# Order of the first transfers in a Fourier-mixing and SoLU kernel on one core: Q and g_ln behind the first pair's x, g_ln loaded in rows, third chunk ahead of the last piece of w_in

## The chip, the cores and the metric

The kernel runs on one core of one Trainium2 chip. The metric is the device time of one execution in microseconds (us), as the median of several runs. Engines are named as in the profile: PE (TensorE, with PEld for its weight loads), DVE (VectorE), ACT (ScalarE), POOL (GpSimd), SP (SyncE). SP and POOL issue the transfers; in the profile "SPq" is SP's queue and "POOLq" POOL's.

## The reference, cut to what matters

```python
# x: (8, 3136, 256), w_in: (256, 1024), w_out: (1024, 256), g_ln: (1024,), all float32
X = np.fft.fft(np.fft.fft(x, axis=1), axis=2).real          # Fourier mixing over sequence and features
h = X.reshape(25088, 256) @ w_in
e = np.exp(h - h.max(-1, keepdims=True))
solu = h * e / (e.sum(-1, keepdims=True) + 1e-9)
ln = (solu - solu.mean(-1)) / sqrt(var(solu) + 1e-6) * g_ln
out = ln @ w_out
```

## The kernel before, in words

The kernel treats two sequences at a time, so there are four pairs. The sequence transform of 3136 points is split into 49 x 64. Its first step (`transform1`, line 215) multiplies rows of x, folded by their symmetries, with the table F. The half-results go through DRAM (`keep` writes `zd`, `turn` reads it back as `g`), and the second step (`transform2`, line 243) uses the table T. The feature transform is not made on the data. It is multiplied into w_in once at the start: with Q, the 256 x 257 table of the feature transform, `product_in` (line 685) makes Wi = Q x w_in in PSUM and `keep_in` (line 689) copies it out. The column `w_mid` comes from `mid` (line 676: two ScalarE copies that read Q's last column) and a third product.

After that, 100 units (25 per pair) run through `up` (line 279), `even`, `join`, `expo`, `product`, `square`, a turn of blocks and the down product (line 462). This loop takes the span from about 58 us to the end.

All of the program's order is written out by hand (`tc.manual_schedule`): the calls in the main function are the order of each engine's instructions. A tile framework only adds the waits. The start, which the change touches, is as follows.

- **The first pair's x.** It comes in 8 chunks of four columns. For chunk c, `load` issues two transfers: `xa` from SP (line 126, 98 rows of 4 KB, 392 KB) and the mirrored rows `xb` from POOL (line 128, a gather by the index table `idx`, as large). Chunks 0, 1, 6 and 7 use two rotating buffers; chunks 2 to 5 lie in "rooms", tiles that serve another purpose later, so that their transfers can start at once. `add_mirror` (lines 143 and 145) adds xb to xa on VectorE, `fold` (lines 150, 151, 163) folds the features into `y` (two buffers), and `transform1` then runs on TensorE in two steps of four matmul passes, each with a ScalarE copy (line 218).
- **w_in in four pieces.** The weights are given to the chip as 32-bit words of wider numbers in this program: a piece of 128 x 4 KB (`piece_in`, line 581, 512 KB) is turned into float32 by `exponent_in` (line 584 on VectorE, then `confine`, three ScalarE steps at lines 608, 610, 612) and `narrow_in` (lines 584, 625, 628, 634 on VectorE). Pieces 0 to 3 must all be converted before the first product with Q.
- **w_out** is treated likewise later (`load_out` line 700, `exponent_out`, `narrow_out`), with g_ln multiplied in at line 634. g_ln is scaled by 2^-20 in `scale_out` (line 704, ScalarE).
- **The queue.** Transfers that SP issues run in order on one queue, those that POOL issues on another. SP has eight completion counters that it uses in turn, so the issue of a transfer also waits for the one issued eight places earlier. SP's order at the start is: idx, piece 0, piece 1, xa of chunk 0, F, piece 2, chunk 1, piece 3, chunk 2, chunk 3, Q, g_ln, chunk 4, chunk 5, chunk 6, then stores, x0, chunk 7 and w_out as they become due.

On VectorE the order in the first 50 us is: exponents of pieces 0 and 1, narrowing of 0 and 1, exponent of 2, chunk 0, narrowing of 2, exponent of 3, chunk 1, narrowing of 3, chunks 2 to 7, then w_out. On TensorE it is: chunks 0 to 3, the product with Q for the even half (8 steps), chunk 4, a quarter of the odd half's product, chunk 5, another quarter, chunks 6 and 7, the rest. Before chunk 3's transform ScalarE does `mid` and `scale_out`.

Of the kernel before, what the change touches and what calls it, by code (L numbers as in the profile page):

```python
# [9 lines left out]
FP32 = mybir.dt.float32  # L10
# [7 lines left out]
P = 128  # L18


N1, N2 = 49, 64
NK = N1 // 2 + 1
NH = N2 // 2
PR = 2 * N1
ZR = 4 * NK
CH = 4
NC = NH // CH
# [11 lines left out]
def shared(b, n):  # L39

    return WHOLE // 2 <= b < n - 1 and all(u % NK for u in (2 * b, 2 * b + 1))
# [3 lines left out]
def kernel(  # L45
# [19 lines left out]
    nc = tc.nc  # L65
    B, S, D = x.shape
    FF = moe_w_in.shape[1]
    KF = FF // P
# [4 lines left out]
    x_g = x.rearrange("b (n1 g l) d -> (b n1 g) (l d)", n1=N1, l=CH)  # L73
    x_pn = x.rearrange("b (n1 n2) d -> (b n1) n2 d", n2=N2)
# [3 lines left out]
    xpool = ctx.enter_context(tc.tile_pool(name="xpool", bufs=2))  # L78
# [6 lines left out]
    fpool = ctx.enter_context(tc.tile_pool(name="fpool", bufs=2))  # L85
# [3 lines left out]
    F = const.tile([PR, 6, ZR], FP32, name="F")  # L89
# [6 lines left out]
    ident = const.tile([P, P], FP32, name="ident")  # L96
    neg_half = const.tile([P, 2], FP32, name="neg_half")
    idx = const.tile([P, NP * (NC + NK)], I32, name="idx")
    w_mid = const.tile([P, FF], FP32, name="w_mid")
    g_ln = const.tile([P, KF], FP32, name="g_ln")  # L100
# [17 lines left out]
    def load(pr, c, room=None):  # L118

        r = slice(pr.p * PR, (pr.p + 1) * PR)  # L120
        if room is None:
            xa = xpool.tile([PR, CH, D], FP32, tag="xa", name="xa")
            xb = xpool.tile([PR, CH, D], FP32, tag="xb", name="xb")
        else:
            xa, xb = (t.rearrange("p (l d) -> p l d", d=D) for t in room)
        nc.sync.dma_start(out=xa, in_=x_pn[r, c * CH + 1 : (c + 1) * CH + 1, :])
        i = pr.p * NC + c
        nc.gpsimd.indirect_dma_start(
            out=xb.rearrange("p l d -> p (l d)"), out_offset=None, in_=x_g,
            in_offset=bass.IndirectOffsetOnAxis(ap=idx[0:PR, i : i + 1], axis=0))  # L130
        x0 = None
        if c == NC - 1:
            x0 = xpool.tile([PR, 1, D], FP32, tag="x0", name="x0", bufs=1)
            nc.sync.dma_start(out=x0, in_=x_pn[r, 0:1, :])
        pr.raw[c] = (xa, xb, x0)

    def add_mirror(pr, c, engine, part=None):

        xa, xb, _ = pr.raw[c]
        rows = (0, CH) if part is None else (part * CH // 2, (part + 1) * CH // 2)  # L140
        r = slice(rows[0], min(rows[1], CH - 1 if c == NC - 1 else CH))
        a, rb = xa[:, r, :], xb[:, ::-1, :][:, r, :]
        i = engine.tensor_tensor(out=a[:, :, 1:D], in0=a[:, :, 1:D], in1=rb[:, :, D - 1 : 0 : -1], op=ALU.add)
        if part is None:
            engine.tensor_tensor(out=a[:, :, 0:1], in0=a[:, :, 0:1], in1=rb[:, :, 0:1], op=ALU.add)
        return i
# [6 lines left out]
    def fold(pr, c):  # L153

        xa, _, x0 = pr.raw.pop(c)
        pr.y[c] = xpool.tile([PR, CH, D], FP32, tag="y", name="y")
        sides = [(pr.y[c], xa)]
        if c == NC - 1:
            pr.y0 = xpool.tile([PR, 1, D], FP32, tag="y0", name="y0", bufs=1)
            sides.append((pr.y0, x0))  # L160
        for o, i in sides:
            fold_features(o, i)
            nc.vector.tensor_copy(out=o[:, :, 0:129:128], in_=i[:, :, 0:129:128])  # L163
# [473 lines left out]
    class Weights:  # L637
# [24 lines left out]
        def load_tables(self):  # L662
            self.Q = fpool.tile([P, KD, D + 1], FP32, tag="ev", name="Q", bufs=1)
            nc.sync.dma_start(out=self.Q, in_=q_tab.rearrange("(c p) d -> p c d", p=P))
            nc.sync.dma_start(out=g_ln, in_=moe_g_ln.rearrange("(c p) -> p c", p=P))

        def load_table(self, i):
            k1 = slice(KG, NK) if i else slice(0, KG)
# [32 lines left out]
                                  in_=moe_w_out.bitcast(I32).rearrange("(c p) f -> p c f", p=P)[:, c])  # L701

        def scale_out(self):
            nc.scalar.mul(out=g_ln, in_=g_ln, mul=2.0 ** -20)

        def exponent_out(self, i):
            self.units.append(exponent(moe_w_out, self.raw[:, 2 * i * NW : 2 * (i + 1) * NW]))
# [76 lines left out]
    with tc.manual_schedule():  # L784
        pairs = [Pair(p) for p in range(NP)]
        first, weights = pairs[0], Weights()
# [3 lines left out]
        rooms = {}  # L790
        for c in range(2, 6, 2):
            room = fpool.tile([P, 2, KF, 4, 64], FP32, tag="uT", name="room", bufs=2)
            room = room[0:PR].rearrange("p w c i m -> p (w c i m)").rearrange("p (a n) -> p a n", a=4)
            rooms[c], rooms[c + 1] = [room[:, i] for i in (0, 1)], [room[:, i] for i in (2, 3)]
        weights.load_in()
        for c in range(4):
            weights.piece_in(c)
            if c:
                load(first, c - 1, rooms.get(c - 1))
            if c == 1:  # L800
                nc.sync.dma_start(out=F, in_=f_tab)
        load(first, 3, rooms[3])
        weights.load_tables()
        for c in range(4, 6):
            load(first, c, rooms[c])
        nc.vector.memset(ones, 1.0)
        nc.vector.memset(neg_half, -0.5)
        bits(top_bit, neg_half[:, 0:1].bitcast(I32), 31, ALU.logical_shift_right, 31, ALU.logical_shift_left)
# [6 lines left out]
        for c in range(NC):  # L815

            if c == 0:
                weights.narrow_in(0)
                weights.narrow_in(1)
            elif c < 3:  # L820
                weights.narrow_in(c + 1)
            if c < 2:
                weights.exponent_in(c + 2)
            add_mirror(first, c, nc.vector)
            fold(first, c)
            if c == NC - 1:
                for i in range(2):
                    weights.exponent_out(i)
                confine(weights.units[0], True)
                weights.narrow_out(0)  # L830
            if c + 6 < NC:
                load(first, c + 6)
            if c == 3:
                weights.place_out()
                for i in range(2):
                    weights.load_out(i)
                weights.load_table(0)
                weights.mid()
                weights.scale_out()
            for s in range(CH // 2):  # L840
                if c == NC - 1:
                    confine(weights.units[0], parts=(s,))
                transform1(first, c * CH // 2 + s)
            if c == 3:
                weights.keep_in(0, weights.product_in(0))
            elif c == 4:
                odd = weights.product_in(1, (0,))
            elif c == 5:
                weights.product_in(1, (1,), odd)
# [136 lines left out]
        for i in range(whole + 1, len(units) + lag + 1):  # L986
# [84 lines left out]
            if i in (len(units), len(units) + 1):  # L1071
                w = i - len(units)
# [7 lines left out]
def _tables(B, S, D):  # L1080

    import numpy as np

    def cs(num, den):
        a = 2.0 * math.pi * (num % den) / den
        return np.cos(a), np.sin(a)

    n1, k1 = np.arange(N1)[:, None], np.arange(NK)[None, :]
    c, s = cs(n1 * k1, N1)
    cm, sm = cs((n1 - N1 // 2) * k1, N1)  # L1090
    zero = np.zeros_like(c)
    tabs = [(c, s), (s, -c), (c, zero), (s, zero), (zero, cm), (zero, sm)]
    f = np.zeros((2, N1, 6, NK, 2, 2))
    for t, (u, v) in enumerate(tabs):
        for b in range(2):
            f[b, :, t, :, b, 0], f[b, :, t, :, b, 1] = u, v
    k = (np.arange(NK)[:, None] + N1 * np.arange(N2)[None, :])[None]
    n2 = (np.arange(NH) + 1) % NH
    c, s = cs(n2[:, None, None] * k, S)
    t = np.stack([c, -s])  # L1100
    t[1, -1] = 1.0 - 2.0 * (k[0] % 2)
    m, d = np.arange(D)[:, None], np.arange(D)[None, :]
    q = np.where(d <= D // 2, cs(m * d, D)[0], -cs(m * (d - D // 2), D)[1])

    q = np.concatenate([q, q[:, D // 2 : D // 2 + 1]], axis=1)
    q[:, D // 2] = 0.0
    sign = np.where(np.arange(P) == 0, 1.0, -1.0)[:, None]
    row = np.arange(B)[:, None] * N1 + np.arange(N1)[::-1]

    load = row.reshape(-1, PR, 1) * (N2 // CH) + N2 // CH - 1 - np.arange(NC)  # L1110
    mirror = np.zeros((P, B // 2 * (NC + NK)), np.int32)
    mirror[:PR, : B // 2 * NC] = load.transpose(1, 0, 2).reshape(PR, -1)
    rows = np.arange(B)[:, None, None] * S + (N1 - np.arange(NK)) + N1 * np.arange(N2)[::-1, None]
    rows = rows.reshape(B // 2, P, NK).transpose(1, 0, 2).reshape(P, -1)
    for b in range(rows.shape[1] // 2):
        if shared(b, rows.shape[1] // 2):

            two = rows[:, 2 * b : 2 * b + 2].reshape(2, 2, 32, 2).transpose(1, 0, 3, 2)
            rows[:, 2 * b : 2 * b + 2] = two.reshape(2, P).T
    mirror[:, B // 2 * NC :] = rows  # L1120
    return {
        "f_tab": f.reshape(PR, 6, ZR).astype(np.float32),
        "t_tab": t.reshape(2 * NH, NK, N2).astype(np.float32),
        "q_tab": q.astype(np.float32),
        "sign": sign.astype(np.float32),
        "mirror": mirror,
    }
# [32 lines left out]
```

## Time and profile before

| | us |
|---|---|
| median of 3 runs | 1126.72 (1125.56 to 1128.06) |
| the profiled execution, its own time | 1127.41 |
| its span, first to last instruction | 1125.6 |
| TensorE busy | 1093.1 (97%) |
| VectorE busy | 980.5 (87%) |
| ScalarE busy | 798.2 (71%) |
| GpSimd busy | 807.5 (72%) |

Times in the profile count from the span's start. A line of the timeline gives start, duration, engine, source line, operation, the tile written and the tile read, how many instructions are merged, and in brackets how long the engine was idle before and what ended the idle time. A line of the waits gives the engine, the tile and line that waited, what ended the wait, the total in us, how often, and the longest.

### The profile page before, as it was taken

What the parts mean: (1) busy time and instruction counts of PE and PEld (TensorE: products, weight loads), DVE (VectorE), ACT (ScalarE), POOL (GpSimd) and SP (SyncE); (2) the same over time, 40 slices, a digit from 0 to 9 for tenths busy, and PEclk for the clock granted to TensorE, in tenths of its full rate; (3) what the DMA queues carried; (4) which work ended last, traced back from release to release, by engine and by line L of the source; (5) the groups of instructions that cost most, each with busy time, mean ns of one, the idle gap of its engine ahead of it and who ended that gap; (6) DMA issues with size and microseconds to landing.
All of it is one profiled execution on the core that took longest, in us unless ns stands there. A gap on an engine that the chain in (4) does not pass through costs nothing. (4 is left out here: it accounts for less than half of the span.)

```text
span 1125.6 us, 22002 instructions
## 1 busy us (share of the span) xinstructions
PE 1093.1 (97%) x7030; PEld 874.1 (78%) x7030; DVE 980.5 (87%) x1440; ACT 798.2 (71%) x1946; POOL 807.5 (72%) x707
## 2 busy tenths in 40 slices
PE   1999999999999999999999999999999999999998
PEld 1556888787787787878877787878877788778888
DVE  6899889888889888898888988898988899888984
ACT  3578777777766777777767777777776777777771
POOL 3048888776887888865878788876776676766665
PEclk9999999999999999999999999999999999999999
DMA  9773798766978889766889797876786785865665
GB/s 236 211 205 82 172 188 202 175 148 152 176 174 167 194 181 187 195 146 144 158 165 183 173 192 181 200 179 143 154 154 143 141 163 125 157 144 112 142 133 126
DMA packets 458569, 185.77 MB, mean 165 GB/s; under 512 B 425774, under 2 KB 440374, under 8 KB 458456
## 3 DMA queue, kind: packets, MB, share of 16 engines
q1 hardware_dynamic: 444568, 145.96, 62.3%
q0 software_dynamic: 13888, 38.42, 13.2%
q8 instruction: 57, 0.93, 0.4%
q14 instruction: 56, 0.46, 0.1%
HBM read 44.78 MB, written 38.80 MB: 74 GB/s over the span
## 5 line engine op out<-in xcount | busy, mean ns | idle before, releaser
L279 PE MATMUL ps_h<-Wi,q 128*128 128x512 f32 x800 | 361.6, 593 | 0.5 <-DVE nmax L300 0.2
L455 POOL TENSOR_TENSOR S<-uT 128x512 f32<-128x512 f32 x186 | 237.3, 1276 | 107.1 <-DVE u L315 35.8
L462 PE MATMUL ps_m<-Ws,S 128*128 128x128 f32 x2304 | 296.0, 275 | 0.0
L462 PEld LDWEIGHTS ps_m<-Ws,S 128*128 128x128 f32 x2304 | 279.5, 192 | 3.2 <-issue 0.2
L322 ACT ACTIVATE h<-u,usum 128x1024 f32<-128x1024 f32 x196 | 225.0, 1148 | 72.3 <-DVE u L315 72.3
L279 PEld LDWEIGHTS ps_h<-Wi,q 128*128 128x128 f32 x800 | 144.2, 190 | 145.0 <-issue 141.9
L315 DVE SCALAR_TENSOR_TENSOR u<-h,u 128x1024 f32<-128x1024 f32 x196 | 233.8, 1228 | 10.9 <-ACT u L308 10.8
L308 ACT ACTIVATE u<-h,nmax 128x1024 f32<-128x1024 f32 x196 | 223.3, 1141 | 2.3 <-DVE nmax L300 1.1
L386 DVE STREAM_TRANSPOSE v<-u 128x2048 f32<-128x2048 f32 x88 | 203.4, 2311 | 3.1
L462 PE MATMUL ps_m<-Wo,uT 128*128 128x128 f32 x1536 | 203.7, 276 | 0.0
L462 PEld LDWEIGHTS ps_m<-Wo,uT 128*128 128x128 f32 x1536 | 187.9, 192 | 1.2 <-issue 1.2
L300 DVE CUSTOM_DVE_ANT_0 h<-ev,ps_h 128x1024 f32<-128x1024 f32 x100 | 122.1, 1221 | 17.1 <-DVE ev L292 9.2
L549 POOL DMA_INDIRECT out_dram<-ot,idx x96 | 111.1, 1157 | 30.0 <-issue 12.8
L300 DVE CUSTOM_DVE_ANT_0 h<-h,ps_h 128x1024 f32<-128x1024 f32 x96 | 117.2, 1221 | 14.6 <-DVE nmax L300 0.7
L455 POOL TENSOR_TENSOR S<-uT,S 128x512 f32<-128x512 f32 x93 | 118.8, 1277 | 7.2
L455 POOL TENSOR_TENSOR S<-S,uT 128x512 f32<-128x512 f32 x93 | 118.6, 1276 | 7.3
L292 DVE SCALAR_TENSOR_TENSOR ev<-w_mid,r,ps_h 128x1024 f32<-128x1024 f32 x99 | 122.8, 1241 | 0.9 <-PE ps_h L279 0.7
L462 PE MATMUL ps_m<-Ws,uT 128*128 128x128 f32 x768 | 101.8, 276 | 0.0
L462 PE MATMUL ps_m<-Wo,S 128*128 128x128 f32 x768 | 101.4, 275 | 0.0
L215 PE MATMUL ps_m<-y,F 98*100 98x258 f32 (+3 forms) x288 | 72.7, 388 | 25.9 <-DVE y L163 24.2
L243 PEld LDWEIGHTS ps_m<-T,g 128*128 128x128 f32 x400 | 60.1, 191 | 47.3 <-issue 45.7
L497 ACT ACTIVATE ot<-ps_m,rs 128x256 f32<-128x256 f32 x96 | 45.4, 473 | 70.4 <-PE ps_m L462 50.4
(109 smaller groups left out, 1232.1 us busy)
## 6 DMA issues: line engine op xcount, KB each, us to landing
uT<-v SPq DMA_DIRECT2D x752, 128.0 KB
g<-zd POOLq DMA_DIRECT2D x72, 160.0 KB, 5.0
out_dram<-ot SPq DMA_DIRECT2D x176, 64.0 KB
xa<-in_x_dram SPq DMA_DIRECT2D x28, 392.0 KB
zd<-z SPq DMA_DIRECT2D x24, 400.0 KB
raw_in<-in_moe_w_in_dram SPq DMA_DIRECT2D x4, 512.0 KB
raw_out<-in_moe_w_out_dram SPq DMA_DIRECT2D x2, 1024.0 KB
room<-in_x_dram SPq DMA_DIRECT2D x4, 392.0 KB
```

What stands on the lines that cost most here:

```text
L215: nc.tensor.matmul(o[..., cs], F[:, 2 * t + h, :], i[..., cs], start=first, stop=True, skip_group_check=True)
L243: nc.tensor.matmul(o, g[:, k, h * P : (h + 1) * P], table, start=(h == 0), stop=True, skip_group_check=True)
L279: nc.tensor.matmul(ps[:, fs], t.q[:, c * P : (c + 1) * P], Wi[:, c, fs], start=True, stop=not whole_even)
L292: nc.vector.scalar_tensor_tensor(out=t.ev, in0=w_mid, scalar=t.r, in1=ps, op0=ALU.mult, op1=ALU.add)
L300: nc.vector.tensor_tensor_reduce(out=t.h[s], in0=t.h[0] if s else t.ev, in1=t.odd, scale=1.0 if s else -0.5, scalar=3.0e38, op0=ALU.add, o ...
L308: nc.scalar.activation(out=t.u[s], in_=t.h[s], func=ACT.Exp, bias=t.nmax[:, s : s + 1], scale=-1.0, accum_out=t.esum[:, s : s + 1])
L315: t.last = nc.vector.scalar_tensor_tensor(out=t.u[s], in0=t.h[s], scalar=-1.0, in1=t.u[s], op0=ALU.mult, op1=ALU.mult, accum_out=t.usum[:, ...
L322: nc.scalar.activation(out=t.h[s], in_=t.u[s], func=ACT.Square, bias=t.usum[:, s : s + 1], scale=-float(FF), accum_out=t.ssq[:, s : s + 1])
L386: nc.vector.transpose(out=t.batch.v[:, :, t.w], in_=t.both.rearrange("p s (g n) -> p (s g) n", n=32))
L455: i = engine.tensor_tensor(out=S[j], in0=a, in1=b, op=op)
L462: nc.tensor.matmul(o, a[:, c], b[:, c], start=start and c == 0, stop=c == n - 1, skip_group_check=True)
L549: dma = nc.gpsimd.indirect_dma_start(out=out, out_offset=bass.IndirectOffsetOnAxis(ap=idx[:, i : i + 1], axis=0), in_=t.ot[s], in_offset=None)
```

## The change

Four things are done. SP's order becomes: idx, piece 0, piece 1, chunk 0, F, gain, piece 2, chunk 1, chunk 2, piece 3, chunk 3, chunk 4, chunk 5, Q, chunk 6. The vector g_ln, before a transfer of 128 x 8 single elements, is loaded as 8 rows of 128 (`load_gain`), turned by one TensorE transpose ahead of chunk 3's transform and scaled by ScalarE from PSUM into the same tile. `mid`, which reads Q, moves behind chunk 3's transform. On VectorE the exponent of piece 2 moves behind the mirror sum of chunk 0, the exponent of piece 3 behind that of chunk 2, and the narrowing of piece 3 behind the fold of chunk 2. `load` and the index table get room for 128 rows, of which 98 are used as before.

```diff
@@ load
+        rows = PR
         if room is None:
-            xa = xpool.tile([PR, CH, D], FP32, tag="xa", name="xa")
-            xb = xpool.tile([PR, CH, D], FP32, tag="xb", name="xb")
+            xa = xpool.tile([P, CH, D], FP32, tag="xa", name="xa")
+            xb = xpool.tile([P, CH, D], FP32, tag="xb", name="xb")
...
-            in_offset=bass.IndirectOffsetOnAxis(ap=idx[0:PR, i : i + 1], axis=0))
+            out=xb[0:rows].rearrange("p l d -> p (l d)"), out_offset=None, in_=x_g,
+            in_offset=bass.IndirectOffsetOnAxis(ap=idx[0:rows, i : i + 1], axis=0))
+        xa, xb = xa[0:PR], xb[0:PR]
@@ class Weights
             nc.sync.dma_start(out=self.Q, in_=q_tab.rearrange("(c p) d -> p c d", p=P))
-            nc.sync.dma_start(out=g_ln, in_=moe_g_ln.rearrange("(c p) -> p c", p=P))
+
+        def load_gain(self):
+            self.gain = fpool.tile([P, D], FP32, tag="ot1", name="gain", bufs=3)[0:KF, 0:P]
+            nc.sync.dma_start(out=self.gain, in_=moe_g_ln.rearrange("(c p) -> c p", p=P))
...
         def scale_out(self):
-            nc.scalar.mul(out=g_ln, in_=g_ln, mul=2.0 ** -20)
+            ps = result(2)[:, 0:KF]
+            nc.tensor.matmul(ps, self.gain, ident[0:KF, 0:KF], is_transpose=True, start=True, stop=True)
+            nc.scalar.mul(out=g_ln, in_=ps, mul=2.0 ** -20)
@@ main
-        for c in range(4):
-            weights.piece_in(c)
-            if c:
-                load(first, c - 1, rooms.get(c - 1))
-            if c == 1:
-                nc.sync.dma_start(out=F, in_=f_tab)
-        load(first, 3, rooms[3])
+        weights.piece_in(0)
+        weights.piece_in(1)
+        load(first, 0)
+        nc.sync.dma_start(out=F, in_=f_tab)
+        weights.load_gain()
+        weights.piece_in(2)
+        for c in range(1, 6):
+            load(first, c, rooms.get(c))
+            if c == 2:
+                weights.piece_in(3)
         weights.load_tables()
-        for c in range(4, 6):
-            load(first, c, rooms[c])
...
-            elif c < 3:
-                weights.narrow_in(c + 1)
-            if c < 2:
-                weights.exponent_in(c + 2)
+            elif c == 1:
+                weights.narrow_in(2)
             add_mirror(first, c, nc.vector)
+            if c in (0, 2):
+                weights.exponent_in(2 + c // 2)
             fold(first, c)
+            if c == 2:
+                weights.narrow_in(3)
...
-                weights.mid()
                 weights.scale_out()
...
             if c == 3:
+                weights.mid()
                 weights.keep_in(0, weights.product_in(0))
@@ _tables
+    mirror[PR:, :NC] = np.arange(PR, P)[:, None] * (N2 // CH) + N2 // CH - 1 - np.arange(NC)
```

More of the change, by code (lines that the diff above doesn't have):

```diff
@@ L120, in load @@
         r = slice(pr.p * PR, (pr.p + 1) * PR)
+        rows = PR
         if room is None:
-            xa = xpool.tile([PR, CH, D], FP32, tag="xa", name="xa")
-            xb = xpool.tile([PR, CH, D], FP32, tag="xb", name="xb")
+            xa = xpool.tile([P, CH, D], FP32, tag="xa", name="xa")
+            xb = xpool.tile([P, CH, D], FP32, tag="xb", name="xb")
         else:
             xa, xb = (t.rearrange("p (l d) -> p l d", d=D) for t in room)
-        nc.sync.dma_start(out=xa, in_=x_pn[r, c * CH + 1 : (c + 1) * CH + 1, :])
+        nc.sync.dma_start(out=xa[0:rows], in_=x_pn[r.start : r.start + rows, c * CH + 1 : (c + 1) * CH + 1, :])
         i = pr.p * NC + c
         nc.gpsimd.indirect_dma_start(
-            out=xb.rearrange("p l d -> p (l d)"), out_offset=None, in_=x_g,
-            in_offset=bass.IndirectOffsetOnAxis(ap=idx[0:PR, i : i + 1], axis=0))
+            out=xb[0:rows].rearrange("p l d -> p (l d)"), out_offset=None, in_=x_g,
+            in_offset=bass.IndirectOffsetOnAxis(ap=idx[0:rows, i : i + 1], axis=0))
+        xa, xb = xa[0:PR], xb[0:PR]
         x0 = None
@@ L792 @@
             room = fpool.tile([P, 2, KF, 4, 64], FP32, tag="uT", name="room", bufs=2)
-            room = room[0:PR].rearrange("p w c i m -> p (w c i m)").rearrange("p (a n) -> p a n", a=4)
+            room = room.rearrange("p w c i m -> p (w c i m)").rearrange("p (a n) -> p a n", a=4)
             rooms[c], rooms[c + 1] = [room[:, i] for i in (0, 1)], [room[:, i] for i in (2, 3)]
         weights.load_in()
-        for c in range(4):
-            weights.piece_in(c)
-            if c:
-                load(first, c - 1, rooms.get(c - 1))
-            if c == 1:
-                nc.sync.dma_start(out=F, in_=f_tab)
-        load(first, 3, rooms[3])
+        weights.piece_in(0)
[8 more added lines that the diff above has]
+                weights.piece_in(3)
         weights.load_tables()
-        for c in range(4, 6):
-            load(first, c, rooms[c])
         nc.vector.memset(ones, 1.0)
```

## The prediction

> **What bounds the kernel now.** I read the page's busy table and slices first, then the table of stretches, the waits, and the timeline of the first 60 us, which holds every edit. TensorE is busy for 97% of the span, and between 100 and 1118 us for 1016.33 of 1018 us, so only what comes before the unbroken run of matmuls can be won or lost.
>
> ```profile
> PE 1093.1 (97%) x7030; PEld 874.1 (78%) x7030; DVE 980.5 (87%) x1440; ACT 798.2 (71%) x1946; POOL 807.5 (72%) x707
> DMA  9773798766978889766889797876786785865665
> ```
>
> The first slices of the DMA row are nearly full: the start is fed by a saturated queue. The waits of VectorE and of the SP queue (first 60 us) say which transfers somebody waited for:
>
> ```profile
> DVE S L584 <- DMA raw_in<-in_moe_w_in_dram: 7.7, 4, 3.2
> DVE room L143 <- DMA room<-in_x_dram: 2.2, 1, 2.2
> SPq L223 <- DMA Q<-in_q_tab_dram: 3.1, 1, 3.1
> ```
>
> In the timeline (start, duration, engine, line, result; bracket: idle before) come the landings and the start of the dense run:
>
> ```profile
> 11.91 16.60 SPq L126 DMA_DIRECT2D room<-in_x_dram  x2
> 15.66 0.43 DVE L584 TENSOR_SCALAR S<-raw_in 128x512 int32<-128x512 int32 x1 [3.18 <-DMA raw_in<-in_moe_w_in_dram]
> 23.50 0.43 DVE L584 TENSOR_SCALAR S<-raw_in 128x512 int32<-128x512 int32 x1 [2.37 <-DMA raw_in<-in_moe_w_in_dram]
> 31.71 6.41 PE L215 MATMUL ps_m<-y,F 98*100 98x258 f32 x16 [1.34 <-DVE y L163]
> 36.37 1.22 DVE L143 TENSOR_TENSOR room<-room 98x1020 f32<-98x1020 f32 x1 [2.21 <-DMA room<-in_x_dram]
> 37.96 3.60 PE L685 MATMUL wps<-w_in,Q 128*128 128x512 f32 x8
> 41.39 1.89 PE L215 MATMUL ps_m<-y,F 98*100 98x258 f32 x8
> ```
>
> The reader is to see that TensorE works without a break from 31.71 us; that the product with Q starts at 37.96, right behind chunk 3's transform; and that from there to 56 us TensorE is busy all the time (18.00 of 18 us between 38 and 56). **What moves the end is when this product starts and how fast the clock is then.** VectorE's lead later on is worth nothing: at 43.3 and 45.9 us it already waits for TensorE.
>
> **What the skill says.** The Trainium skill, DMA: Bandwidth & Descriptors, Rules for kernel authors: a last dimension that isn't contiguous lowers to one descriptor per element. The trace agrees: g_ln, 4 KB, makes some 1,000 packets under 512 B between 29 and 33 us, while the SP queue moves 0.03 MB/us; and SP's issue right behind it (11.91 us above) is held for 16.1 us. Same page, Queues, rings and completion order: each DMA engine takes turns between queues. Between 8 and 28 us SP's queue holds a third to two thirds of the engines' time in nearly every us, and the gathers on POOL's queue the rest. TensorE: Matmul & The Clock Gate, Part 1: matmuls run at half the clock until TensorE was busy for a free-running window of some 3.4 us. Here L215 issues every 428 ns until 36.9 us and every 214 ns from 37.3 us, 5.6 us after the stretch began at 31.7 us; a burst from 26.64 to 30.37 us did not raise it. The page's PEclk row doesn't show this.
>
> **The change, part by part.**
>
> *Queue order.* SP's queue is served in order. Before: piece 2 of w_in, chunk 1's xa, piece 3, chunk 2, chunk 3, Q, g_ln, chunk 4, chunk 5. After: gain, piece 2, chunk 1, chunk 2, piece 3, chunk 3, chunk 4, chunk 5, Q. The landings before, from who waited: piece 2 15.66, piece 3 23.50, chunk 3 31.1 (SP issues x0 at 31.10 on it), Q 34.55, chunk 4 36.4, chunk 5 37.65 (SP's second w_out issue at 37.67). Chunk 1 and piece 3, 904 KB, took 7.84 us: 115 KB/us beside the gathers; chunks 2 and 3, 784 KB in 7.6 us, 103 KB/us. So after: chunk 1 at 15.7 + 392/115 = 19.1, chunk 2 at about 22.7, piece 3 at 27.3 (3.8 later than before). Up to chunk 3 the bytes are the same: **31.1, unchanged.**
>
> *VectorE.* Narrowing piece 1 ends at 12.47. The gather of chunk 0 lands at 2.89 + 10.9 = 13.8, so its mirror sum (1.25) runs ahead of piece 2's exponent, then exponent (0.34) from 15.7 and fold (1.5): y0 at 17.5, before 18.75. Narrow piece 2 (2.59): 20.2. Chunk 1 (2.5): 22.7, before 26.6. Mirror of chunk 2: 24.0. Then it waits 3.3 us for piece 3 at 27.3; exponent and fold: y2 at 29.0, before 31.57. Narrow piece 3 (2.59): 31.6; chunk 3 (2.69): **y3 at 34.3, before 34.16.** The 3 us gained on the way are given back at piece 3. Behind the new wait stand y2 and TensorE; gathers 6 and 7 on POOL are set off 2 to 4 us earlier, behind the same queue of gathers.
>
> *TensorE.* Chunk 2's transform runs 29.0 to 32.4 (8 x 428 ns), idles 1.9 us, and chunk 3's runs 34.3 to 37.7. The gain transpose stands in the idle: no row shows it; nearest are L403 (0.12 us each in a row) and L269 (0.19), so 0.1 to 0.4 us and nothing on the path; gain lies ready from some 12 us. Its ScalarE copy replaces one of 0.20 us. The two mid copies (0.69 together) now wait for Q, and only the product's own copy stands behind them.
>
> *Q.* Chunk 4, chunk 5, Q and g_ln had landed by 37.65. Without g_ln's packets (half to one us) it is 36.7 to 37.1. Against that, chunks 4 and 5 in packets of 4 KB now meet the last two gathers, where Q's rows of 1 KB met them before: 250 to 280 ns a 4 KB packet instead of some 200, over up to 14 packets, up to one us. **Q at 36.7 to 38.6, taken 37.9.** Q and g_ln were never late before (34.55 against 37.96), so taking them out of the way has that slack to spend, and spends it.
>
> *Start and clock.* The product starts at 37.9 to 38.0 against 37.96: 0 (-0.8 to +0.6). But TensorE's stretch now begins at 34.3, 2.6 us later. Counted alike, the clock rises at 37.3 + 2.6 = 39.9 and the product runs 2.0 us at half speed: **+1.0** (0 to +1.7, since the window runs freely).
>
> *At nothing:* SP no longer hangs for 16.1 us, but chunks 4 and 5 were limited by the wire and x of chunk 6 (39.2) by the bytes ahead; first w_out issue moves from 36.52 to about 37.7, covered, since VectorE takes it at 47.66 without waiting and the engines fall idle by 46 us; tiles of 128 partitions with 98 rows used, and new table rows that no gather reads, change no transfer (still 98x1024). What is late next is Q.
>
> Sum: 1127.4 of the profiled execution (span 1125.6 and 1.8 around it) + 1.0 = 1128.4; the runs' median lies 0.7 under that execution: **1127.7.** About 0.2%, 2.25 us, is what a measurement of this kernel can tell from no change.
>
> **The rivals.** *A, Q after the transform, and the clock starts over* (slower): place, the product with Q; price, from the point where Q lands later than chunk 3's transform ends (37.7). With Q at 38.5 the stretch counts from there, the clock rises at about 44.1, and 6.5 of 8 steps take 858 ns: it ends at 44.8 instead of 41.4, +3.3: 1130.0. For it: the burst of 3.7 us that raised nothing. Against: a gap of tenths may not count. *B, the wire gets faster* (faster): with SP free and 1,000 tiny packets gone, 0.25 MB/us hold from 24 us on where 0.20 were seen. Then 5 us at 0.05 are 0.25 MB, 1 us of all queues; chunk 3 lands at 29.5, Q at 35.5, and with piece 3 at 26 y3 is ready at 33. With the clock up at the next window the product starts at 35.6: -2.4, 1124.3. Against: big packets beside gathers took 250 to 300 ns whatever Q did. *C, all hidden*: both ends move by under half a us, 1126.7.
>
> **How the numbers follow.** Forecast 0.42 (1126.5 to 1129.2; a tenth of it beyond 0.2% slower), A 0.32 (nine tenths beyond), B 0.18 (nine tenths beyond 0.2% faster), C 0.08. Slower 0.04 + 0.29, with late matters such as w_out 0.36; faster 0.16; within 0.48. Range: down to B's 1124.3, up to A's 1130.4.
>
> **What would show it.** Right: VectorE idle some 3 us for raw_in near 27 us; y3 near 34; L685 starting at 37.5 to 38.5 with steps of about 850 ns at first; SP with no issue over 1 us before 30 us. Wrong: L685 starting before 37 us, or at 214 ns steps in chunk 3's transform (B); an idle before L685 released by Q and slow steps past 42 us (A); anything after 60 us that differs by itself.

## The result and the profile after

| | before | after |
|---|---|---|
| median of 17 runs each, us | 1126.87 (1125.52 to 1128.23) | 1129.39 (1127.17 to 1132.28) |
| ratio to before, 95% interval | | 1.0024 (1.0016 to 1.0032) |
| profiled execution, its own time, us | 1127.41 | 1128.60 |
| its span, us | 1125.6 | 1126.8 |

The changed kernel is slower by 0.24%, 2.5 us in the medians. Its profiled execution is one of its shorter runs: it shows 1.2 us of the loss. The runs also spread more here, over 5.1 us instead of 2.7; in the comparisons of the experiments below the kernel before itself spread over 5.1 to 7.3 us, so the wider spread isn't shown to come from the change.

The busy times of the kernel after, from its page:

```profile
PE 1094.9 (97%) x7031; PEld 874.6 (78%) x7031; DVE 980.6 (87%) x1440; ACT 798.6 (71%) x1946; POOL 805.9 (72%) x707
```

TensorE is busy for 1.8 us more with one instruction more (the transpose, 0.27 us). Most of it is the same work done at a slower clock: in the lines below, the product takes 1.04 us more, and the transforms of chunks 2 and 3 take 3.28 + 3.71 us instead of 6.41. The waits of the kernel after, first VectorE's, then the SP queue's (first 60 us; engine, line that waited, what ended it; total, times, longest):

```profile
DVE S L586 <- DMA raw_in<-in_moe_w_in_dram: 6.2, 4, 3.0
...
DVE room L145 <- DMA room<-in_x_dram: 0.5, 1, 0.5
```

```profile
SPq L136 <- DMA raw_in<-in_moe_w_in_dram: 4.0, 1, 4.0
```

VectorE's waits for w_in are shorter in sum (6.2 against 7.7 us), yet one of 3.0 us now stands behind chunk 2. The timeline of the kernel after shows where, and that Q is now waited for:

```profile
7.15 5.22 SPq L127 DMA_DIRECT2D room<-in_x_dram  x3
...
12.42 0.40 SPq L666 DMA_DIRECT2D Q<-in_q_tab_dram  x1
...
23.08 1.22 DVE L145 TENSOR_TENSOR room<-room 98x1020 f32<-98x1020 f32 x1 [0.47 <-DMA room<-in_x_dram]
...
27.39 0.43 DVE L586 TENSOR_SCALAR S<-raw_in 128x512 int32<-128x512 int32 x1 [3.02 <-DMA raw_in<-in_moe_w_in_dram]
...
37.57 0.62 PEld L690 LDWEIGHTS wps<-w_in,Q 128*128 128x128 f32 x2 [0.28 <-DMA Q<-in_q_tab_dram]
```

SP has issued everything up to Q by 12.8 us; in the kernel before, the issue of chunk 4 behind g_ln alone took 16.1 us. Piece 3 lands at 27.39. The weight load that needs Q waits for it until 37.57. TensorE alone, kernel after:

```profile
22.67 3.73 PE L217 MATMUL ps_m<-y,F 98*100 98x258 f32 x8 [1.43 <-DVE y L165]
29.25 3.28 PE L217 MATMUL ps_m<-y,F 98*100 98x258 f32 x8 [2.84 <-DVE y L165]
32.45 0.27 PE L710 MATMUL ps_m<-ident,gain 8*128 8x8 f32 x1
34.35 3.71 PE L217 MATMUL ps_m<-y,F 98*100 98x258 f32 x8 [1.63 <-DVE y L165]
37.85 4.64 PE L690 MATMUL wps<-w_in,Q 128*128 128x512 f32 x8
42.32 1.89 PE L217 MATMUL ps_m<-y,F 98*100 98x258 f32 x8
...
58.29 1.05 PE L245 MATMUL ps_m<-T,g 128*128 128x128 f32 x8
```

The product (L690) starts 0.1 us earlier than before but takes 4.64 us instead of 3.60. The second step's first matmul stands at 58.29. In the kernel before:

```profile
57.36 1.05 PE L243 MATMUL ps_m<-T,g 128*128 128x128 f32 x8
```

From there to the end of the span it is 1068.5 us in the kernel after and 1068.2 in the one before. **Of the 1.2 us that this execution lost, 0.9 lie ahead of that point.** Behind it the profiled executions of all kernels of this study differ by up to 1.5 us (1067.9 to 1069.4), whatever their start was. Most of that comes from the output stores at the end: from the start of TensorE's last group of matmuls to the end of the span it is 5.6 to 7.1 us.

*Why the product is slower* is read from the table of stretches, cut into pieces of 3.4 us counted back from the moment at which the trace records the rise of the clock. Columns: stretch, us, then busy us and instructions of PE, PEld, DVE, ACT, POOL, then PEclk, DMA share, GB/s. Before, with the rise at 37.27 us:

```profile
27.00:30.40 3.40, 3.37 (x8) 1.79 (x7) 3.34 (x6) 0.58 (x1) 0.00 (x0) 1.00 1.03 197
30.40:33.90 3.50, 2.19 (x5) 1.57 (x6) 3.47 (x7) 0.74 (x2) 0.00 (x0) 1.00 0.93 209
33.90:37.30 3.40, 3.40 (x9) 2.32 (x8) 1.19 (x3) 1.84 (x6) 0.00 (x0) 1.00 0.89 270
```

After, with the clock up at 26.28, down at 29.69 and up at 39.93:

```profile
22.90:26.30 3.40, 3.40 (x8) 1.92 (x8) 1.30 (x2) 0.59 (x1) 0.00 (x0) 1.00 1.00 231
26.30:29.70 3.40, 0.56 (x3) 0.42 (x3) 2.27 (x6) 2.37 (x4) 0.00 (x0) 1.00 0.91 204
29.70:33.10 3.40, 3.02 (x8) 1.63 (x6) 3.34 (x6) 1.51 (x4) 0.00 (x0) 0.50 0.91 219
33.10:36.50 3.40, 2.15 (x5) 1.57 (x6) 3.27 (x7) 0.24 (x3) 0.00 (x0) 0.50 0.92 239
36.50:39.90 3.40, 3.40 (x7) 1.87 (x6) 3.37 (x8) 1.65 (x4) 0.00 (x0) 0.50 0.96 289
```

In these tables a stretch with TensorE busy from end to end is followed by the full clock; one busy for 3.02 or 3.37 us is not; one busy for 0.56 us is followed by half the clock. (PEclk stands at 1.00 ahead of the first recorded change although the steps take 428 ns there, so go by the steps.) The changes of one trace lie whole multiples of 3.41 us apart (here 1 and 3 of them). The Trainium skill, TensorE: Matmul & The Clock Gate, Part 1: The HAM clock gate, gives a free-running window of 3413 ns; these numbers agree.

Busy from end to end is necessary in all the traces of this study, but not sufficient. Four windows that the record shows as full raised nothing: those that begin at 17.64 and 34.70 us in e3, at 35.14 in e4 and at 17.88 in e11 (the experiments below). In each, TensorE's work had begun 0.00 to 0.14 us ahead of the window; wherever the clock rose, it had begun at least 0.20 us ahead (22.67 against 22.87 us in the change is the closest). So work seems to need a lead of 0.14 to 0.20 us by the record's times; why isn't shown.

In the kernel before, the first such window inside the stretch begun at 31.71 us ends at 37.27, just ahead of the product. In the kernel after, VectorE's wait for piece 3 leaves TensorE idle for 2.84 us ahead of chunk 2, and the narrowing of piece 3, which now stands between the two chunks on VectorE, for 1.63 us ahead of chunk 3. The clock that chunk 1 had raised is lost again, and the next full window ends 2.1 us into the product.

### The profile page after: what moved, and what is told of

Read it like the earlier page. It is cut to its first block, busy times and chain, and to the rows that moved or that the text cites. A ratio compares the mean times of both kernels' runs of the same rounds, so it can differ in the third digit from the quotient of the medians.

```text
span 1126.8 us, 22003 instructions
## 1 busy us (share of the span) xinstructions
PE 1094.9 (97%) x7031; PEld 874.6 (78%) x7031; DVE 980.6 (87%) x1440; ACT 798.6 (71%) x1946; POOL 805.9 (72%) x707
```

## The experiments

All medians are in us; each ratio is to the kernel before, run beside it. The experiments were measured in three groups on three chips (e1 to e4, e5 to e8, e9 to e11), in which the median of the kernel before was 1127.04, 1126.77 and 1125.83. Across the groups compare ratios, not medians. Theory 1 says that the loss is the clock at the product with Q, because VectorE's new order leaves TensorE idle between chunks 2 and 3. Theory 2 says that Q behind chunk 5 sets the start. Theory 3, that the loss lies elsewhere. Several kernels fill idle time of TensorE with matmuls of ones by ones whose result nobody reads (each makes two instructions):

```diff
+    def fill(n):
+        w = ps_h.tile([P, FF], FP32, tag="h0", name="warm")
+        for _ in range(n):
+            nc.tensor.matmul(w[:, 0:P], ones, ones, start=True, stop=True)
```

### e1_after_fill: the idle time between chunks 2 and 3 filled

In the kernel after, behind the transform of chunk c:

```diff
+            if c == 2:
+                fill(5)
```

> The changed kernel with five matmuls that nobody reads (128x128 ones by ones, into a PSUM tile that the product with Q overwrites later) between chunk 2's transform and the gain transpose, so that TensorE does not idle from 32.5 to 34.3 us. Theory 1 (the clock: TensorE's unbroken stretch begins later, so its clock rises only inside or after the product with Q): the stretch now begins at 29.2 us, the clock rises by 36 us, the product of 8 steps takes 3.6 us from about 37.9 us and the median falls to 1126.5 to 1127.5. Theory 2 (Q is late on the wire): the product starts when it did, the fill changes nothing, 1129.4. Theory 3 (something after 60 us): 1129.4.

1127.15 (1124.94 to 1132.07), ratio 1.0008 (0.9995 to 1.0021). In its profile the clock rises at 34.75 us, ahead of chunk 3, and the product starts at 37.23 and takes 3.67 us. In this execution the filling gives back what the change lost. The interval overlaps that of the change (1.0016 to 1.0032), so the median alone doesn't settle it, and single runs are as long as the longest of the change: the filling may not work in all of them.

### e2_before_fill: the idle time of the kernel before filled

In the kernel before, at the same place:

```diff
+            if c == 1:
+                fill(3)
```

> The kernel before with three such unread matmuls between chunk 1's and chunk 2's transform, so that TensorE works without a break from 26.6 us. Theory 1: the clock rises by 33.5 us, chunk 3's transform ends at about 36.1 instead of 37.9 us, the product with Q starts there (Q landed at 34.6) and the median falls by 1.5 to 2 us to about 1125. Theory 2: Q was in time, nothing else binds, 1126.9. Theory 3: 1126.9.

1126.28 (1123.80 to 1129.66), ratio 0.9995 (0.9986 to 1.0003). The clock rises at 30.27 us, the product starts at 34.99 and the span is 2.0 us shorter, as expected of one execution. The median does not confirm it: a miss.

### e3_q_late: Q, g_ln and the queue as changed, the order of the conversions as before

The kernel after, with VectorE's block of the kernel before and, in the loop of loads:

```diff
-            if c == 2:
+            if c == 1:
                 weights.piece_in(3)
```

> The changed kernel with piece 3 and VectorE's order put back as before (piece 3 ahead of chunk 2); Q still behind chunk 5 and g_ln still in rows. Theory 1: TensorE's stretch begins at 31.7 us again, the clock rises as before, the product starts at 37.9: 1126.5 to 1127.3. Theory 2: the loss stays, 1129 or more. Theory 3: undecided.

1130.06 (1129.55 to 1133.31), ratio 1.0042 (1.0026 to 1.0058). Theory 1 as it stood fails: with the old order on VectorE the kernel is slower still. TensorE's timeline of this kernel says why:

```profile
30.24 3.71 PE L217 MATMUL ps_m<-y,F 98*100 98x258 f32 x8 [1.34 <-DVE y L165]
33.88 0.27 PE L710 MATMUL ps_m<-ident,gain 8*128 8x8 f32 x1
34.70 3.73 PE L217 MATMUL ps_m<-y,F 98*100 98x258 f32 x8 [0.55 <-ACT g_ln L711]
38.23 5.24 PE L690 MATMUL wps<-w_in,Q 128*128 128x512 f32 x8
```

The transpose of the gain (L710) writes the PSUM tile that chunk 3's first step needs. That step now waits 0.55 us for ScalarE's g_ln copy; the unbroken stretch begins at 34.70 instead of 30.24. The window that begins at the same moment doesn't count, so the clock rises only at 41.53, and the product takes 5.24 us. In the change this wait can't be seen, because the transpose falls into idle time that the reordering made.

### e4_reorder: the order of the conversions alone

The kernel before, with VectorE's block of the kernel after and piece 3 behind chunk 2 on SP's queue:

```diff
+        weights.piece_in(2)
+        load(first, 1)
+        load(first, 2, rooms[2])
+        weights.piece_in(3)
         load(first, 3, rooms[3])
```

> The kernel before with only piece 3 behind chunk 2 and VectorE's order of the change; Q and g_ln as before. Theory 1: the stretch begins at 34.3 us, Q (34.6 us) is early, the product starts at 37.8 with a clock that is still low: 1129 to 1129.8, all of the loss. Theory 2: Q is in time, so no loss: 1126.9.

1127.92 (1126.79 to 1130.62), ratio 1.0007 (1.0001 to 1.0014). TensorE's timeline of its profiled execution, which is its longest run:

```profile
29.81 3.70 PE L215 MATMUL ps_m<-y,F 98*100 98x258 f32 x8 [2.82 <-DVE y L163]
35.05 3.71 PE L215 MATMUL ps_m<-y,F 98*100 98x258 f32 x8 [1.53 <-DVE y L163]
38.54 5.30 PE L685 MATMUL wps<-w_in,Q 128*128 128x512 f32 x8
```

Nearly the same two idle times as in the change (2.84 and 1.63 us), and the clock rises at 41.96: the stretch began 0.09 us ahead of a window, which was too little for that window, so it took one more. The reordering costs 0.07%, about 0.8 us: a part of the loss, and less than was expected. The rest needs Q's place or the gain. The theories were therefore split. In the expectations from here on, 1a stands for the gain's PSUM tile, and 1b (in e9: 1c) for a late Q that leaves TensorE idle right before the product.

### e5_after_warm: all the idle time up to chunk 3 filled, the gain turned first

The kernel after, with `scale_out` moved from chunk 3 to ahead of chunk 0, and:

```diff
+            if c in {1: 7, 2: 8}:
+                fill({1: 7, 2: 8}[c])
```

> The changed kernel with the gain transpose moved ahead of chunk 0's transform and unread matmuls (7 between chunks 1 and 2, 8 between chunks 2 and 3) that leave no idle of TensorE from 22.7 to about 32 us in any run. Theory 1 (all of the loss is the clock's state at the product with Q): the clock has risen by 29.5 us in every run, chunk 3's transform takes 1.9 us, and the product of 3.6 us starts when Q lands, at about 37.6 us: 0.3 us better than before, median 1126.3 to 1127, and a narrower spread than the changed kernel's 5 us. Theory 2 (Q's landing itself costs some 2 us): 1129.

1128.10 (1126.07 to 1133.13), ratio 1.0015 (1.0006 to 1.0025); expected was about the time before. TensorE's timeline and the table of stretches of this kernel:

```profile
33.70 1.94 PE L217 MATMUL ps_m<-y,F 98*100 98x258 f32 x8 [1.33 <-DVE y L165]
37.53 5.37 PE L690 MATMUL wps<-w_in,Q 128*128 128x512 f32 x8 [1.89 <-DMA Q<-in_q_tab_dram]
```

```profile
35.50:38.90 3.40, 1.51 (x5) 0.69 (x5) 3.37 (x7) 1.28 (x3) 0.00 (x0) 1.00 0.97 271
39.00:42.20 3.20, 3.20 (x5) 1.19 (x4) 1.67 (x4) 0.00 (x0) 0.00 (x0) 0.50 1.03 368
42.40:50.00 7.60, 7.60 (x32) 5.11 (x31) 5.05 (x14) 4.00 (x7) 0.00 (x0) 1.00 0.60 201
```

The clock was up from 28.69 us, and chunk 3's transform took 1.94 us. TensorE then idled 1.89 us for Q, the window was left with 1.51 us of work, and the clock fell at 38.93 for one window, within the product: 5.37 us instead of 3.60. This is the mechanism of the prediction's rival A in a profile: Q behind the transform, and the clock starts over. Here the filling brought it about, by ending chunk 3's transform about two us before Q lands; no trace shows it in the change itself.

### e6_q_late_early_gain: e3 with the gain turned ahead of chunk 0

On top of e3:

```diff
+            if c == 0:
                 weights.scale_out()
```

> As e3 (changed kernel, piece 3 and VectorE's order as before), with the gain transpose ahead of chunk 0's transform, so that chunk 3's transform no longer waits 0.55 us for g_ln's copy to free its PSUM bank. Theory 1a (that bank wait broke TensorE's stretch in e3): the stretch runs unbroken from 30.2 us into the product, median 1126.8 to 1128, some 2 us below e3. Theory 1b (the break is the wait for Q): it stays near 1130.

1127.70 (1125.30 to 1130.15), ratio 1.0010 (0.9999 to 1.0020), against 1.0042 with the gain at chunk 3. In TensorE's timeline chunks 2 and 3 stand together again:

```profile
30.76 5.87 PE L217 MATMUL ps_m<-y,F 98*100 98x258 f32 x16 [1.28 <-DVE y L165]
36.49 3.70 PE L690 MATMUL wps<-w_in,Q 128*128 128x512 f32 x8
```

The intervals lie apart, so the shared PSUM tile is the larger part of e3's loss. The runs fall into two groups, seven up to 1126.82 and seven from 1128.58 on; only one of the first group was profiled. What the second does is not shown.

### e7_after_q_early: the change with Q ahead of chunks 4 and 5

In the kernel after, inside the loop of loads:

```diff
-        weights.load_tables()
+            if c == 3:
+                weights.load_tables()
```

> The changed kernel with Q loaded right behind chunk 3 instead of behind chunk 5; all else as changed. Theory 1b (waiting for Q breaks the stretch in a part of the runs): Q lands near 34.5 us, the stretch is unbroken from chunk 3's transform on, the longest runs (1130 to 1132) go and the median falls to about 1128, as e4. Theory 1a: no break there, 1129.4 as changed.

1128.08 (1125.38 to 1132.03), ratio 1.0012 (1.0003 to 1.0020). TensorE's timeline:

```profile
35.25 1.94 PE L217 MATMUL ps_m<-y,F 98*100 98x258 f32 x8 [1.25 <-DVE y L165]
37.03 3.60 PE L690 MATMUL wps<-w_in,Q 128*128 128x512 f32 x8
...
57.87 1.16 PE L245 MATMUL ps_m<-T,g 128*128 128x128 f32 x8 [1.15 <-DMA g<-zd]
```

With Q in time the product follows chunk 3 at once, at full clock. Then 1.15 us are lost to another wait: the second step waits for the half-results coming back from DRAM. The loss is half that of the change (0.12% against 0.24%), though the intervals just overlap. The expectation that the longest runs would go is a miss: the longest, 1132.03, is as long as the longest of the change.

### e8_before_fill6: e2 with twice the filling

In the kernel before:

```diff
+            if c in {1: 6}:
+                fill({1: 6}[c])
```

> The kernel before with six unread matmuls between chunk 1's and chunk 2's transform instead of e2's three, since in e2's profile 0.3 us of idle was left there. Theory 1: unbroken from about 26 us in every run, so the clock has always risen by 33 us, chunk 3's transform ends near 36 us and the product starts there: 1124.5 to 1125.3 with few runs above 1126. If the clock isn't the cause: 1127.

1126.36 (1123.81 to 1128.49), ratio 0.9997 (0.9990 to 1.0004): no gain, a miss like e2. The profiled product starts at 36.69 us, 1.3 us earlier than before.

### e9_after_bridged: e5 with the wait for Q filled as well

On top of e5:

```diff
-            if c in {1: 7, 2: 8}:
-                fill({1: 7, 2: 8}[c])
+            if c in {1: 7, 2: 8, 3: 7}:
+                fill({1: 7, 2: 8, 3: 7}[c])
```

> As e5 (changed kernel, early gain transpose, unread matmuls between chunks 1, 2 and 3), with seven more unread matmuls between chunk 3's transform and the product with Q. In e5's profile TensorE idled 1.9 us for Q and the clock fell to half at 38.9 us, so that the product took 5.4 us. Theory 1c (the wait for Q lets the clock fall or not rise): bridged, the product starts when Q lands, about 37.5 us, and takes 3.6 us in every run; median 1126.2 to 1127, no run above 1129. Theory 2 (something else than the clock): 1128.1 as e5.

1127.01 (1125.36 to 1129.53), ratio 1.0008 (1.0001 to 1.0015). TensorE's timeline:

```profile
36.19 1.73 PE L794 MATMUL warm<-ones 128*128 128x128 f32 x14
37.98 3.70 PE L690 MATMUL wps<-w_in,Q 128*128 128x512 f32 x8
```

Nothing but work without use was added to e5, and the ratio went from 1.0015 to 1.0008. The intervals overlap, so what the wait for Q costs isn't settled. (The longest run went from 1133.13 to 1129.53 us, but that of the kernel before also went from 1131.00 to 1129.16 between the two groups.) Two runs lie just above the 1129 that was expected as a bound. Against the change itself (1.0016 to 1.0032) the interval lies just apart. e9 is the change with TensorE kept busy and the gain turned early, and two thirds of the loss are gone.

What is left in this execution isn't at the start. The second step begins at 57.48 us and TensorE's last matmuls at 1119.73, each 0.1 us later than in the kernel before, yet the span is 1126.8 us, 1.2 us longer. The last lines of e9, then of the kernel before:

```profile
1119.73 1.06 PE L464 MATMUL ps_m<-Wo,S 128*128 128x128 f32 x8
1122.48 0.96 POOL L551 DMA_INDIRECT out_dram<-ot,idx  x1 [3.44 <-issue]
```

```profile
1119.65 1.06 PE L462 MATMUL ps_m<-Wo,S 128*128 128x128 f32 x8
1121.29 0.96 POOL L549 DMA_INDIRECT out_dram<-ot,idx  x1 [2.18 <-DVE ot L520]
```

GpSimd issues the last store of the output 1.2 us later; why isn't shown.

### e10_best and e11_gain_at3: the gain in rows without the rest of the change

e10 is the kernel before with g_ln loaded in rows behind F and turned ahead of chunk 0, filled as e8:

```diff
                 nc.sync.dma_start(out=F, in_=f_tab)
+                weights.load_gain()
...
+            if c == 0:
                 weights.scale_out()
...
+            if c in {1: 6}:
+                fill({1: 6}[c])
```

> The kernel before with e8's six unread matmuls, g_ln loaded in rows behind F and its transpose ahead of chunk 0's transform; Q, piece 3 and VectorE's order as before. Theory: nothing breaks TensorE's stretch from 26 us, Q is there at 34.6 us or a little earlier, the product starts at 35.5 to 36.5 us at full clock: 1124.8 to 1126, 0.1 to 0.2% better than before. Rival (g_ln's form is worth nothing): as e8, 1126.4.

1125.22 (1123.75 to 1129.37), ratio 0.9999 (0.9989 to 1.0009). Its profiled span is 1123.3 us, the shortest of the study, and its product starts at 35.98. Over its runs it is no faster than the kernel before, whose median beside it is 1125.83: the expected gain of 0.1 to 0.2% is a miss. **No version beats the kernel before by more than can be measured.**

e11 is e10 without the filling and with `scale_out` left at chunk 3, where the change has it:

```diff
-            if c == 0:
                 weights.scale_out()
```

> The kernel before with g_ln loaded in rows behind F and its transpose ahead of chunk 3's transform, as in the change; Q, piece 3 and VectorE's order as before, nothing else. Theory 1a (the transpose's PSUM bank is the one that chunk 3's transform writes next, so TensorE waits 0.5 us for g_ln's copy and its stretch breaks at 35 us): the clock rises after the product has begun in a part of the runs, 1128 to 1129.5. If that break doesn't matter: 1126.5.

1129.98 (1129.04 to 1131.39), ratio 1.0035 (1.0023 to 1.0047). TensorE's timeline, then ScalarE's:

```profile
30.86 3.71 PE L215 MATMUL ps_m<-y,F 98*100 98x258 f32 x8 [1.34 <-DVE y L163]
34.49 0.27 PE L708 MATMUL ps_m<-ident,gain 8*128 8x8 f32 x1
35.89 3.74 PE L215 MATMUL ps_m<-y,F 98*100 98x258 f32 x8 [1.13 <-ACT g_ln L709]
39.42 4.77 PE L688 MATMUL wps<-w_in,Q 128*128 128x512 f32 x8
```

```profile
34.60 0.59 ACT L218 COPY z_v<-ps_m 100x512 f32<-100x512 f32 x1 [1.12 <-PE ps_m L215]
35.08 0.69 ACT L679 ACTIVATE w_mid<-ones,Q 128x128 f32<-128x128 f32 x2
35.68 0.16 ACT L709 ACTIVATE g_ln<-ps_m 128x8 f32<-128x8 f32 x1
```

With a transpose of 0.27 us and a copy of 0.16 us at this place the kernel is 0.35% slower. The copy stands behind chunk 2's copy and the two of `mid`, chunk 3 waits 1.13 us for it. The clock rises at 41.77 us, at the end of the first window that lies wholly behind that wait. This is more than the 1128 to 1129.5 that was expected.

## Why the prediction was right or wrong, point by point

- **Queue order: right.** Chunk 2 was expected at about 22.7 us and was there at 23.08; piece 3 at 27.3, and came at 27.39. Q was taken at 37.9, and the weight load got it at 37.57.
- **VectorE: right.** y0 at 17.5 (TensorE's first transform starts at 17.50), y2 at 29.0 and y3 at 34.3 (the transforms start at 29.25 and 34.35); a wait of 3.3 us for piece 3 (3.02). The 3 us gained on the way are given back there, as the prediction says.
- **TensorE: right for the change, with one dependence missed.** The transpose stands in the idle time and costs nothing there. The prediction looked for its cost in the instruction (0.1 to 0.4 us; it is 0.27) and in ScalarE's copy, and not in the PSUM tile that it shares with chunk 3. Where no idle time covers it, e11 measures 0.35%.
- **At nothing: right.** SP's issues are free by 12.8 us and nothing ends earlier for it. w_out was expected to be issued at about 37.7 and is at 36.60 us, which nothing depends on.
- **Start and clock: right in the profiled execution, too small for the median.** "The product starts at 37.9 to 38.0": 37.85. "The clock rises at … 39.9": 39.93. "+1.0": the product takes 1.04 us more and the span is 1.2 us longer. On the way, unforeseen, the clock had risen at 26.28 and fallen again. The median lost 2.5 us, and this term is the one that was mis-sized: it counted the rise of one execution forward ("counted alike") and added the result to a median. The window's phase is another in each execution: counted in whole windows from the span's start, the changes lie 3.1 us into a window in the kernel before, 2.4 in the change and 0.6 in e1. All phases together give hardly more (1.3 us by the estimate below), so most of what is missing must be something else; the wait for Q, which was kept for rival A, is the candidate that the experiments support.
- **What the median is made of.** The reordering alone costs 0.07% (0.01 to 0.14; e4). An estimate for it: with the phase free, the mean rise shifts with the start of the unbroken stretch, from 31.71 to 34.35 us, and 2.64 us at half speed lose 1.3 us, which lies in e4's interval. Q's place probably brings much of the rest: with Q early 0.12% is left (e7), with all idle time filled except for Q's 0.15% (e5), with that filled too 0.08% (e9). A late Q with the old order of conversions and an early gain costs 0.10% (e6), which its interval (−0.01 to 0.20) doesn't tell from nothing. These intervals overlap, so the division isn't shown.
- **Rivals.** A was called slower with 1130.0 us. Its mechanism is shown in e5's profile (that execution took 1129.68 us); that the longer runs of the change are such executions is argued from it, since only one execution of each kernel has a trace. B, a faster wire, is refuted: chunk 3's transform ran on steps at half speed and the product started at 37.85, not 35.6. C, all hidden, is refuted by the interval, whose lower end is 1.0016.
- **Left open.** Why e2, e8 and e10 start the product 1.3 to 3.0 us earlier in their profiles and gain nothing in the median; and what keeps e9 0.08% above the kernel before. In e9's one trace it is the late last store. In others it may be that the product can't start ahead of Q at 37.5 us, while the kernel before can in runs in which its clock rises early; no trace here shows such a run.

The largest single chance, 0.48, had been given to no measurable difference; the interval of the ratio, 1.0016 to 1.0032, reaches to both sides of 0.2%. The median of 1129.39 us lies above the forecast's own 1126.5 to 1129.2. It is inside the range only because the range was stretched to rival A; the forecast's own sum does not reach it.

## What to carry to other kernels

At the start of a kernel that is later bound by TensorE, read the idle times of TensorE and not the waits of the engine that was improved: here 3 us of earlier data brought nothing, and the short waits that came with them, close to the dense run, cost time. A tiny instruction that borrows a rotating PSUM tile belongs in front of the first user or in a known idle time. And a forecast from one trace of something that depends on a free-running window should be made over all its phases, not by shifting the one rise that the trace happens to show; here that alone gives 1.3 us of the 2.5.

## What the runs showed of the hardware

- The clock's changes within a trace lie a multiple of 3.41 us apart (26.28, 29.69 and 39.93 in the change; 28.69, 38.93 and 42.34 in e5). A window with 3.02 or 3.37 us of work raised nothing; nor did full ones into which the work had a lead of 0.00 to 0.14 us (e3, e4, e11), while a lead of 0.20 us was enough in the change. Windows with 0.06 (e1), 0.56 and 1.51 us dropped the clock, and one with 1.96 us, in e1 from 21.1 to 24.5 us, was not followed by a fall.
- With g_ln in single elements behind Q, the next issue of SP took 16.1 us in the kernel before. In e10 and e11, with g_ln in rows behind F and the rest of the queue as before, the issues of chunks 4 and 5 together took 0.9 us. It brought no landing that decided anything: in e11 VectorE waits for chunk 4 until 36.50 us, as it did before until 36.37.
- The spread of runs is no fixed property of a kernel: the kernel before spread over 2.7 us in one comparison (17 runs) and over 7.3 us in another (65 runs, beside e5, whose 22 runs spread over 7.1).
